# Two half-batch groups per weight tile against one group of up to 512 tokens, in an attention and two-layer MLP kernel

## The chip, the cores and the metric

The kernel runs on one core of one Trainium2 chip. Its time is the device time of one execution in microseconds, the median of three executions. Every matrix product is on TensorE (PE); VectorE (DVE), ScalarE (ACT) and GpSimd (POOL) do the elementwise work, and all transfers are issued from SyncE's queue (SP).

## The reference

Four batches of 576 tokens, eight heads of 64. Causal attention with a decay per position gives 2304 tokens of 512 channels, which two MLP layers take in turn.

```python
scores = scale * (q @ k.T) + cum[:, None] - cum[None, :]     # causal; cum = cumsum(log(f))
x = softmax(scores) @ v                                      # heads side by side: 2304 x 512
x = ((x @ w_a) * (x @ w_b)) @ w_out                          # layer 0; 512 -> 1536 -> 512
xn = x / sqrt(mean(x * x) + 1e-6) * rms_g
out = (silu(xn @ w_gate) * (xn @ w_val)) @ w_out2            # layer 1; 512 -> 1536 -> 512
```

## The kernel before, in words

**Phases.** The MLP is cut into chunks of tokens; before, a chunk is a batch. A phase is one layer on one chunk, and `PHASES` (line 32) lists eight of them as (layer, chunk): (0,0), (0,1), (1,0), (0,2), (1,1), (0,3), (1,2), (1,3). Below, "phase 0" to "phase 7" count along this list. A phase goes through 36 weight tiles (`NG`, line 46): 24 for the two inner products, taken by turns (the first of a pair is gated, the second multiplies it), and 12 for the outer product, three to each of four output blocks. Each layer has 36 tiles, so every phase streams all 36 of its layer again.

**Groups.** A bank of PSUM holds 512 fp32 columns, and a batch has 576 tokens, so each chunk is worked in two groups of tokens: `CUT` (line 23) makes them 256 and 320 for batch 0, 288 and 288 for the others. For one weight tile and one group PE does a *block*: 12 matmuls (`block` in `plan_mlp`, lines 571 to 578), four slices of 128 by three products, because operands are split into a high and a low part (`w[0]*xh + w[0]*xl + w[1]*xh`). Each matmul loads its own weights. A block writes one of `M_BANKS` = 4 banks called `m` (line 62); the bank is free again when ACT or DVE has read it (`gate`, `product`, `out_1`, `out_2`).

**Weight tiles.** A tile is 512 KB. On first use it is loaded as 64-bit words (`raw`), decoded (`weights`, lines 480 to 539: ACT `rebase`, DVE `shift` and `join`, ACT `high`, POOL `low`) and saved to DRAM (`wd`); later uses load the saved form, `w<-wd`, line 496. Both live in a ring of `W_BUFS` = 5 buffers. During phase 1, `EARLY[1]` = 16 tiles of layer 1 are decoded ahead of their phase.

**Attention** of a batch is planned into phases by `ATT` (line 40): batch 2 over phases 1 and 2, batch 3 over phases 3 and 4. Scores go to `S_BANKS` = 2 banks `s` (line 1102, and 1124 for the last 64 rows of two heads together), then softmax, transposes to one bank `t` (line 804), products with V to one bank `pv` (line 1185). Phase 0 starts after a special start-up for the first 256 rows of batch 0, with three banks `bm`.

**Order.** All operations are recorded first and then put in a fixed order per engine by a list scheduler (`Plan.order`, line 212) with costs such as `mm` (line 67) and due times from `block_time`. Each engine then runs its list strictly in order: an instruction that waits holds up all behind it.

Of the kernel before, what the change touches and what calls it, by code (L numbers as in the profile page):

```python
# [9 lines left out]
F32 = mybir.dt.float32  # L10
F32R = mybir.dt.float32r
# [10 lines left out]

CUT = (256, 288, 288, 288)
N0, NMAX = CUT[0], max(max(x, S - x) for x in CUT)
PIECES = sorted({0, S, *CUT})
NEG = -8e9
# [4 lines left out]

PHASES = [(0, 0), (0, 1), (1, 0), (0, 2), (1, 1), (0, 3), (1, 2), (1, 3)]

LAG = 18
SLOT = [0, 1, 2, 0]

EARLY = {0: 1, 1: 16}

# [3 lines left out]
    (1, ALL, ((0, LAG, 99, 1.0),), 2),  # L42
    (2, ALL, ((1, 0, 99, 0.7), (2, 0, 99, 0.5)), 0),
    (3, ALL, ((3, 0, 99, 0.4), (4, 0, 99, 0.5)), 0),
]
# [7 lines left out]

AHEAD = [18000, 20000, 14000, 20000]
BOOT_STEP, EARLY_AT = 3000, 10000
# [5 lines left out]
W_BUFS, W32_BUFS, A_BUFS, BP_BUFS = 5, 2, 4, 4  # L61
S_BANKS, T_BANKS, PV_BANKS, M_BANKS = 2, 1, 1, 4
P_BUFS, PT_BUFS = 4, 4
LANDED, READY, RATE = 980, 230, 360


def mm(n):

    return max(107.0, n / 2.4 + 12.5)

# [15 lines left out]
def dve(n):  # L86
    return 69 + n / 0.96
# [10 lines left out]
def pool1(n):  # L98
    return 55 + n / 0.96
# [6 lines left out]
def half(c, s):  # L106

    return slice(CUT[c] * s, S if s else CUT[c])


def size(c, s):
    return S - CUT[c] if s else CUT[c]


def halves_of(c, a, e):
    return [s for s in range(2) if a < half(c, s).stop and e > half(c, s).start]

# [184 lines left out]
class Kernel:  # L302
# [91 lines left out]
    def make_x(self, pool, s):  # L394
        for t in range(2):
            for k in range(KT):
                self.X[s, t, k] = pool.tile([128, S], F32R, name=f"x{s}{t}{k}")

# [15 lines left out]
    def steps(self, p):  # L414

        both = (0, 1)
        if p:
            return [(j, both) for j in range(NG)]
        ab = 2 * FT
        return (  # L420
            [(j, both[:1]) for j in range(LAG)] + [(j, both) for j in range(LAG, ab)]
            + [(j, both[1:]) for j in range(LAG)] + [(j, both) for j in range(ab, NG)]
        )

    def weave(self):
        np_ = len(PHASES)
        blocks = [sum(len(subs) for _, subs in self.steps(p)) for p in range(np_)]
        extra = [[0.0] * n for n in blocks]
        for c, rows, parts, sf in ATT:
            for p, a, e, share in parts:  # L430
                span = range(a, min(e, blocks[p]))
                for i in span:
                    extra[p][i] += share * sum(self.unit_cost(u, h < sf) for u in rows for h in range(H)) / len(span)

        self.T, t = [], 0.0
        for p in range(np_):
            self.T.append([t])
# [13 lines left out]
        todo, norm = list(ATT), None
        for p, (m, c) in enumerate(PHASES):
            while todo and todo[0][2][0][0] <= p:
                self.plan_attention(*todo.pop(0))
            self.plan_mlp(p, m, c, norm)
            norm = (p, c) if m == 0 else None
# [85 lines left out]
    def plan_mlp(self, p, m, c, norm):  # L542
# [3 lines left out]
        for i_step, (j, subs) in enumerate(self.steps(p)):  # L546
            w = self.weights(m, j, self.block_time(p, k + 1))
            if i_step % 3 != 1:
                for i in early:
                    self.weights(1, i, self.block_time(p, k + 1) + 20000)  # L550
                    break
            if norm and i_step == 0:
                stages = self.plan_norm(*norm)
            if norm and i_step in NORM_STEPS:
                next(stages)
            for s in subs:
# [116 lines left out]
    def out_2(self, acc, c, i, s, e):  # L673
        nc, op = self.nc, self.op
        o, n = self.tile([128, NMAX], "a", A_BUFS), size(c, s)
        t0 = c * S + half(c, s).start
        op(
# [9 lines left out]
    def plan_norm(self, p, c):  # L687
        parts = self.x_parts[1, c] = []
        for s in range(2):
            self.normed(c, s, self.block_time(p + 1, NORM_AT + 4 * s), parts)  # L690
            yield
# [159 lines left out]
    def first_pair(self, i, u, t):  # L851
# [6 lines left out]
        cols = [slice(g * e, g * e + e) for g in range(2)]  # L858
        s = self.bank("bm", 3, (128, 512), self.bpsum)
        p = self.tile([128, 2 * N0], "bP", BP_BUFS, pool=self.bp)  # L860
# [149 lines left out]

    def plan_attention(self, c, rows, spread, sf):
        spans = [(self.T[p][a], self.T[p][min(e, len(self.T[p]) - 1)], share) for p, a, e, share in spread]
        spans[-1] = (spans[-1][0], spans[-1][1] - AHEAD[c], spans[-1][2])

        def place(x):
            for a, b, share in spans:
                if x <= share:
                    break
                x -= share
            return a + (b - a) * x / share  # L1020

        *whole, last = rows
# [4 lines left out]
        after = [n for s in range(2) for n in self.ab_blocks.get((1, 0, s), [])] if c == 3 else []  # L1027
        for hs in zip(range(0, H, 2), range(1, H, 2)):
            f = hs[1] < sf
            tiles = [self.head(c, h, rows[0][0], place(pos / total), f) for h in hs]  # L1030
            groups = [[last], *(whole[i : i + 2] for i in range(0, len(whole), 2))]
            for us in groups:
                pss = []
                for u in us:
# [5 lines left out]
                    pos += 2 * weigh(rows.index(u), u, hs[0])  # L1040
                self.values(c, hs, us, pss, tiles, t, after)

    def head(self, c, h, q0, t, sf):

# [18 lines left out]
        vr = self.tile([128, 5, D], "vr", 4)  # L1063
        load(256 * (S - q0), lambda: qr.tile[0:64, q0:], self.qT[g, :, q0:], writes=[(qr, 0)], dt=15000)
        load(147456, lambda: kr.tile[0:64], self.kT[g], writes=[(kr, 0)], dt=15000)
        for x, i in zip((qb, kb), at):
# [63 lines left out]

    def values(self, c, hs, us, pss, tiles, t, after):

# [45 lines left out]
        def product(x):  # L1178
# [14 lines left out]
        )  # L1193
        late = ["late"] if SLOT[c] == 2 else []
        out = lambda i: self.X[SLOT[c], i, hs[0] // 2][:, a0:e1]
        hi, lo = (("xb", c, i, hs, a0) for i in range(2))
        n = e1 - a0
        op(
            ACT, act(n, 1), lambda: nc.scalar.activation(out(0), pv.tile[:, :n], AF.Copy), reads=[pv, *late], writes=[hi],
            prio=t + 6500, after=after,  # L1200
        )
        op(
            DVE, dve(n),
            lambda: nc.vector.tensor_tensor(out=out(1), in0=pv.tile[:, :n], in1=out(0).bitcast(F32), op=ALU.subtract),
            reads=[pv, hi, *late], writes=[lo], prio=t + 6800, after=after,
        )
        self.x_parts.setdefault((0, c), []).extend([(hi, halves_of(c, a0, e1)), (lo, halves_of(c, a0, e1))])


# [48 lines left out]
```

## Time and profile before

| | us |
|---|---|
| median of three runs | 1142.66 |
| lowest, highest | 1137.82, 1145.03 |
| the profiled execution | 1149.22 |
| its span, first to last instruction | 1147.4 |

The span is cut in stretches below at the phase borders of this execution: start-up to 36, phase 0 to 254, phase 1 to 398, phase 2 to 530, phase 3 to 660, phase 4 to 800, phase 5 to 914.5, phase 6 to 1029.5, phase 7 to the end. A PE matmul's shown duration includes its way through the array and overlaps the next one, so the cost of a matmul is read from the distance between starts.

### The profile page before, as it was taken

Reading aid. Unit: us, or ns where it says so; the run is one execution under the profiler, and the core shown is the slowest. Engines: PE = TensorE matmul, PEld = TensorE weight load, DVE = VectorE, ACT = ScalarE, POOL = GpSimd, SP = SyncE. Lnnn points to the kernel's source line nnn. Section 1 sums busy time; section 2 is a strip of 40 time slices with the busy share of each in tenths; the row PEclk is TensorE's granted clock in tenths of the full one; section 3 lists DMA queues with packets and bytes.
Section 4 is the critical chain, followed back from the end, with each engine's and each line's share of the span. In section 5 each row is a group of like instructions: output and inputs, shape, how many; then the busy total and the mean of one; then the engine's idle time right before and its main releaser. Section 6 shows DMA issues by size and latency. Waiting matters only on the chain.

```text
span 1147.4 us, 22605 instructions
## 1 busy us (share of the span) xinstructions
PE 1129.9 (98%) x8742; PEld 1084.2 (94%) x8742; DVE 562.9 (49%) x1587; ACT 490.3 (43%) x1208; POOL 180.3 (16%) x187
## 2 busy tenths in 40 slices
PE   8999999999999999999999999999999999999998
PEld 7676899999999999999999999999999999999998
DVE  5567757667973469642352268621221166204420
ACT  6677647666663446542342245422222133112210
POOL 2323313432421012441020020200000000000000
PEclk7889999999999999999999999999999999999999
DMA  6768796879797454697455454445555555565553
GB/s 184 241 215 297 275 293 220 265 229 320 251 377 219 142 159 157 224 316 259 148 163 162 149 161 148 141 157 157 169 166 166 166 165 165 170 197 173 166 174 107
DMA packets 77184, 229.82 MB, mean 200 GB/s; under 512 B 11533, under 2 KB 22493, under 8 KB 77077
## 3 DMA queue, kind: packets, MB, share of 16 engines
q1 hardware_dynamic: 77076, 228.38, 61.2%
q8 instruction: 69, 1.13, 0.4%
q14 instruction: 39, 0.31, 0.1%
HBM read 185.21 MB, written 43.13 MB: 199 GB/s over the span
## 4 chain that ended last, share of the span: by engine, by line
PE 86%; DMA 6%; ACT 3%; DVE 2%; issue 1%; POOL 1%; SPq 0%; ACTq 0%; DVEq 0%; POOLq 0%
PE m L576 25%; PE m L578 24%; PE m L577 24%; PE pv L1185 3%; PE t L804 3%; PE s L1102 3%; DMA raw<-wb 2%; PE s L1124 2%; DMA raw<-wo 1%; ACT P L769 1%; DMA kr<-kT 1%; DMA bq<-aux 1%; ACT w L515 1%; DVE w L523 1%; DMA raw<-wv 0%
## 5 line engine op out<-in xcount | busy, mean ns | idle before, releaser
L576 PE MATMUL m<-x,w 128*128 128x288 f32 (+2 forms) x1536 | 462.6, 301 | 0.0
L578 PE MATMUL m<-x,w 128*128 128x288 f32 (+2 forms) x1536 | 453.8, 295 | 0.1
L577 PE MATMUL m<-x,w 128*128 128x288 f32 (+2 forms) x1536 | 453.1, 295 | 0.0
L576 PEld LDWEIGHTS m<-x,w 128*128 128x128 f32 x1536 | 289.4, 188 | 5.1 <-issue 3.0
L577 PEld LDWEIGHTS m<-x,w 128*128 128x128 f32 x1536 | 289.6, 189 | 0.8 <-issue 0.2
L578 PEld LDWEIGHTS m<-x,w 128*128 128x128 f32 x1536 | 289.1, 188 | 0.3 <-POOL w L490 0.3
L576 PE MATMUL m<-g,w 128*128 128x288 f32 (+2 forms) x768 | 229.4, 299 | 0.0
L578 PE MATMUL m<-g,w 128*128 128x288 f32 (+2 forms) x768 | 226.6, 295 | 0.0
L577 PE MATMUL m<-g,w 128*128 128x288 f32 (+2 forms) x768 | 226.3, 295 | 0.0
L634 ACT ACTIVATE g<-a 128x288 fp32r<-128x288 f32 (+2 forms) x192 | 84.7, 442 | 174.0 <-DVE a L618 173.7
L618 DVE TENSOR_TENSOR a<-m,a 128x288 f32<-128x288 f32 (+2 forms) x192 | 87.3, 455 | 125.6 <-PE m L578 119.7
L576 PEld LDWEIGHTS m<-g,w 128*128 128x128 f32 x768 | 144.5, 188 | 1.5 <-issue 1.2
L577 PEld LDWEIGHTS m<-g,w 128*128 128x128 f32 x768 | 144.6, 188 | 0.1
L578 PEld LDWEIGHTS m<-g,w 128*128 128x128 f32 x768 | 144.4, 188 | 0.0
L490 POOL TENSOR_TENSOR w<-w,w 128x512 fp32r<-128x512 f32 x72 | 99.1, 1383 | 208.5 <-ACT w L487 147.5
L600 ACT ACTIVATE a<-m 128x288 f32<-128x288 f32 (+2 forms) x192 | 78.1, 407 | 120.3 <-PE m L578 119.7
L637 DVE TENSOR_TENSOR g<-a,g 128x288 fp32r<-128x288 f32 (+2 forms) x182 | 91.9, 506 | 58.9 <-ACT g L634 58.4
L769 ACT ACTIVATE P<-P,mn 128x512 f32<-128x512 f32 (+4 forms) x128 | 76.3, 597 | 43.5 <-DVE mn L762 42.4
L762 DVE CUSTOM_DVE_ANT_0 P<-s,mask 128x512 f32<-128x512 f32 (+4 forms) x128 | 61.9, 498 | 65.2 <-PE s L1102 46.2
L607 DVE SCALAR_TENSOR_TENSOR a<-a,m 128x288 f32<-128x288 f32 (+1 forms) x96 | 43.1, 452 | 93.7 <-ACT a L600 93.4
L1166 ACT ACTIVATE pt<-t 128x384 f32<-128x384 f32 (+2 forms) x101 | 51.6, 511 | 43.7 <-PE t L804 43.6
L804 PE MATMUL t<-ident,P 128*128 128x128 f32 (+1 forms) x376 | 63.2, 278 | 6.5 <-ACT pt L1166 6.1
(105 smaller groups left out, 1065.8 us busy)
## 6 DMA issues: line engine op xcount, KB each, us to landing
w<-wd SPq DMA_DIRECT2D x251, 512.0 KB
wd<-w SPq DMA_DIRECT2D x72, 512.0 KB
raw<-wo SPq DMA_DIRECT2D x24, 512.0 KB
raw<-wa SPq DMA_DIRECT2D x12, 512.0 KB
raw<-wb SPq DMA_DIRECT2D x12, 512.0 KB
raw<-wg SPq DMA_DIRECT2D x12, 512.0 KB
raw<-wv SPq DMA_DIRECT2D x12, 512.0 KB
vr<-vA SPq DMA_DIRECT2D x32, 128.0 KB
```

The source lines that it names most:

```text
L490: nc.gpsimd.tensor_tensor(out=w.tile[:, 1, :], in0=i32.tile.bitcast(F32), in1=w.tile[:, 0, :].bitcast(F32), op=ALU.subtract)
L576: nc.tensor.matmul(o, w.tile[:, 0, wc], xh, start=kt == 0, stop=False)
L577: nc.tensor.matmul(o, w.tile[:, 0, wc], xl, start=False, stop=False)
L578: nc.tensor.matmul(o, w.tile[:, 1, wc], xh, start=False, stop=kt == last)
L600: ACT, act(n, 1), lambda x: nc.scalar.activation(x[:, :n], acc.tile[:, :n], func, scale=scale),
L618: nc.vector.tensor_tensor(out=a.tile[:, :n], in0=acc.tile[:, :n], in1=a.tile[:, :n], op=ALU.mult)
L634: nc.scalar.activation(out(0), x(), AF.Copy, **({} if scale is None else {"scale": scale}))
L637: self.engine(by).tensor_tensor(out=out(1), in0=x(), in1=out(0).bitcast(F32), op=ALU.subtract)
L762: nc.vector.tensor_tensor_reduce(out=p.tile[:n, i * w : i * w + w], in0=s[i].tile[:n, :w], in1=masks[i][:n], scale=-0.125, scalar=mn.tile[ ...
L769: nc.scalar.activation(o, o, AF.Exp, bias=mn.tile[:n, len(s) - 1 : len(s)], scale=-1.0, accum_out=x[:n])
L804: nc.tensor.transpose(ps.tile[:w, c : c + n], p.tile[:n, i * 128 : i * 128 + w], self.ident[:n, :n])
L1166: nc.scalar.activation(x.tile[:r, :to], ps.tile[:r, :to], AF.Copy)
```

## The change

Batch 0 keeps its two groups. The other 1728 tokens are cut without regard to batches into chunks of 512, 448, 320 and 448, each worked as a single group, so there are ten phases of 36 tiles instead of eight; the (layer, chunk) list is given in the diff. Phases are again counted from 0, so phase 1 is now layer 0 on 512 tokens, and phase 8 layer 1 on 320. Attention of batches 2 and 3 is planned in two parts each and loads only the keys that a part needs; results that fall into two chunks are copied in two pieces (`homes`). There are three `s` banks, three `m` banks and two `bm` banks, instead of two, four and three. The planner's matmul cost and its DMA rate are other numbers, and 14 tiles instead of 16 are decoded early, evenly over phase 1.

```diff
-CUT = (256, 288, 288, 288)
-N0, NMAX = CUT[0], max(max(x, S - x) for x in CUT)
+CHUNKS = [(0, (256, 320)), (576, (512,)), (1088, (448,)), (1536, (320,)), (1856, (448,))]
+WIDTH = [sum(x) for _, x in CHUNKS]
...
-PHASES = [(0, 0), (0, 1), (1, 0), (0, 2), (1, 1), (0, 3), (1, 2), (1, 3)]
+PHASES = [(0, 0), (0, 1), (1, 0), (0, 2), (1, 1), (0, 3), (1, 2), (0, 4), (1, 3), (1, 4)]
...
-SLOT = [0, 1, 2, 0]
-
-EARLY = {0: 1, 1: 16}
+
+SLOT, HAD = [0, 1, 2, 0, 1], {3: 0, 4: 1}
+
+EARLY = {0: 1, 1: 14}
...
-    (2, ALL, ((1, 0, 99, 0.7), (2, 0, 99, 0.5)), 0),
-    (3, ALL, ((3, 0, 99, 0.4), (4, 0, 99, 0.5)), 0),
+    (2, ALL[:3], ((1, 0, 99, 0.6), (2, 0, 99, 0.5)), 0),
+    (2, ALL[3:], ((3, 0, 99, 0.7), (4, 0, 99, 0.4)), 0),
+    (3, ALL[:1], ((4, 18, 99, 1.0),), 0),
+    (3, ALL[1:], ((5, 0, 99, 0.6), (6, 0, 99, 0.5)), 0),
...
-S_BANKS, T_BANKS, PV_BANKS, M_BANKS = 2, 1, 1, 4
+S_BANKS, T_BANKS, PV_BANKS, M_BANKS, BM_BANKS = 3, 1, 1, 3, 2
 P_BUFS, PT_BUFS = 4, 4
-LANDED, READY, RATE = 980, 230, 360
+LANDED, READY, RATE = 980, 230, 320
 
 
 def mm(n):
 
-    return max(107.0, n / 2.4 + 12.5)
+    return max(107.0, 0.4375 * n + 7)
...
-            if i_step % 3 != 1:
+            if p == 1 and (i_step + 1) * EARLY[1] // NG > i_step * EARLY[1] // NG:
...
-        s = self.bank("bm", 3, (128, 512), self.bpsum)
+        s = self.bank("bm", BM_BANKS, (128, 512), self.bpsum)
```

What moves is shown at three places. The first is PE in a phase without attention, at the border between two blocks; `m` is the bank written, `x` the activations, `w` the weight tile. Before, in the last phase (layer 1, batch 3):

```order
L576 MATMUL m2142_12993<-x003_115,w2141_12870 128x288
L577 MATMUL m2142_12993<-x013_119,w2141_12870 128x288
L578 MATMUL m2142_12993<-x003_115,w2141_12870 128x288
L576 MATMUL m2144_13011<-x000_112,w2141_12870 128x288
L577 MATMUL m2144_13011<-x010_116,w2141_12870 128x288
L578 MATMUL m2144_13011<-x000_112,w2141_12870 128x288
```

and with the change in phase 8:

```order
L591 MATMUL m2123_11058<-x003_115,w2119_10993 128x320
L592 MATMUL m2123_11058<-x013_119,w2119_10993 128x320
L593 MATMUL m2123_11058<-x003_115,w2119_10993 128x320
L591 MATMUL m2126_11077<-x000_112,w2125_11011 128x320
L592 MATMUL m2126_11077<-x010_116,w2125_11011 128x320
L593 MATMUL m2126_11077<-x000_112,w2125_11011 128x320
```

Before, the weight tile stays for a second block; now each block has a new tile.

The second place is SP's queue in phase 1, where stored tiles of layer 0 (`w<-wd`), raw tiles of layer 1, saves (`wd<-w`) and loads of attention heads go out by turns. Before:

```order
L496 DMA w_3921<-wd_9_147 128x1024
L512 DMA raw_3926<-wv 128x512
L528 DMA wd_6_180<-w_3910 128x1024
L496 DMA w_4002<-wd_10_148 128x1024
L496 DMA w_4046<-wd_11_149 128x1024
L512 DMA raw_4061<-wg 128x512
```

and with the change, at the same stored tiles:

```order
L511 DMA w_3696<-wd_9_147 128x1024
L511 DMA w_3718<-wd_10_148 128x1024
L527 DMA raw_3739<-wg 128x512
L511 DMA w_3742<-wd_11_149 128x1024
L543 DMA wd_3_177<-w_3752 128x1024
L511 DMA w_3786<-wd_12_150 128x1024
```

At the same point of the phase three fewer saves have gone out; the early tiles are spread further back.

The third place is PE at the start, at the first scores (`bm`) and the idle matmuls that fill waits (`warm`). Before:

```order
L817 MATMUL warm_212<-spun 128x128 x13
L868 MATMUL bm_242<-bk,bq 128x128 x2
L868 MATMUL bm_250<-bk,bq 128x256 x2
L868 MATMUL bm_264<-bk,bq 128x128 x2
L868 MATMUL bm_271<-bk,bq 128x256 x2
```

and with the change:

```order
L832 MATMUL warm_212<-spun 128x128 x13
L883 MATMUL bm_242<-bk,bq 128x128 x2
L883 MATMUL bm_250<-bk,bq 128x256 x2
L883 MATMUL bm_264<-bk,bq 128x128 x2
L832 MATMUL warm_212<-spun 128x128
L883 MATMUL bm_276<-bk,bq 128x256 x2
```

The fourth pair of scores now stands behind an idle matmul, since its bank is one that an earlier pair used.

## Rows read from the trace of the kernel before

**Rows 1.** The page: span, PE, and granted PE clock in 40 slices.

```profile
span 1147.4 us, 22605 instructions
PE 1129.9 (98%) x8742; PEld 1084.2 (94%) x8742; DVE 562.9 (49%) x1587; ACT 490.3 (43%) x1208; POOL 180.3 (16%) x187
PEclk7889999999999999999999999999999999999999
```

**Rows 2.** Stretches by phase: busy us (instructions) per engine, clock, DMA share, GB/s.

```profile
36.00:254.00 218.00, 210.16 (x1634) 182.35 (x1634) 144.59 (x440) 140.28 (x340) 70.50 (x71) 0.97 0.78 256
254.00:398.00 144.00, 142.68 (x1148) 138.61 (x1148) 91.49 (x261) 79.02 (x196) 38.27 (x37) 1.00 0.77 262
398.00:530.00 132.00, 130.74 (x1029) 128.77 (x1027) 82.26 (x205) 67.12 (x155) 42.30 (x38) 1.00 0.67 226
...
800.00:914.50 114.50, 114.50 (x867) 114.50 (x866) 24.29 (x53) 26.12 (x64) 0.00 (x0) 1.00 0.54 168
```

**Rows 3.** Timeline of PE, phase 2: start us, duration us; first matmuls of successive blocks.

```profile
500.11 0.28 PE L576 MATMUL m<-g,w 128*128 128x256 f32 x1
...
501.55 0.31 PE L576 MATMUL m<-g,w 128*128 128x320 f32 x1
...
503.31 0.28 PE L576 MATMUL m<-g,w 128*128 128x256 f32 x1
```

**Rows 4.** Timeline of PE: four score matmuls in a row, twice, and what follows.

```profile
289.31 0.40 PE L1102 MATMUL s<-ka,qa 128*128 128x512 f32 x1
...
290.24 0.30 PE L576 MATMUL m<-x,w 128*128 128x288 f32 x1
...
775.86 0.34 PE L1102 MATMUL s<-ka,qa 128*128 128x384 f32 x1
...
776.57 0.29 PE L576 MATMUL m<-g,w 128*128 128x288 f32 x1
```

**Rows 5.** PE's waits in the whole span: us in total, times, longest.

```profile
PE t L804 <- ACT pt L1166: 6.1, 7, 1.5
PE s L1124 <- POOL ka L1049: 2.4, 2, 1.6
...
PE s L1102 <- DVE mn L762: 0.4, 2, 0.2
```

**Rows 6.** Stretches chosen by DMA load; columns as in rows 2.

```profile
60.00:230.00 170.00, 164.09 (x1318) 144.71 (x1315) 116.04 (x353) 110.38 (x270) 51.87 (x51) 0.99 0.80 262
254.00:350.00 96.00, 95.41 (x763) 92.75 (x763) 76.16 (x208) 63.77 (x154) 32.53 (x29) 1.00 0.88 308
320.00:335.00 15.00, 15.00 (x133) 14.35 (x132) 10.35 (x29) 9.36 (x23) 3.86 (x3) 1.00 1.02 417
```

**Rows 7.** Waits of SP's queue in the whole span: the longest.

```profile
SPq L496 <- PE m L578: 469.2, 180, 5.1
```

**Rows 8.** Timelines of PE, ACT and DVE, end of phase 2's inner products.

```profile
487.16 0.31 PE L578 MATMUL m<-x,w 128*128 128x320 f32 x1
...
490.51 0.28 PE L576 MATMUL m<-g,w 128*128 128x256 f32 x1
...
489.52 0.67 ACT L515 ACTIVATE w<-raw 128x512 f32<-128x512 f32 x1 [2.16 <-DMA raw<-wo]
490.09 0.42 ACT L600 ACTIVATE a<-m 128x320 f32<-128x320 f32 x1
...
490.54 0.49 DVE L607 SCALAR_TENSOR_TENSOR a<-a,m 128x320 f32<-128x320 f32 x1 [1.35 <-ACT a L600]
```

**Rows 9.** Groups by line in phase 2: busy, mean ns, idle before, releaser.

```profile
L515 ACT ACTIVATE w<-raw 128x512 f32<-128x512 f32 x18 | 12.1, 674 | 20.4 <-DMA raw<-wo 17.3 <-DMA raw<-wv 2.3 <-DMA raw<-wg 0.8
```

**Rows 10.** Timeline of the end: the last matmul and the last copy.

```profile
1143.85 0.29 PE L578 MATMUL m<-g,w 128*128 128x288 f32 x1
...
1144.23 0.41 ACT L678 ACTIVATE a<-m 128x288 f32<-128x288 f32 x1 [1.18 <-PE m L578]
```

More of the change, by code (lines that the diff above doesn't have):

```diff
@@ L21 @@
 KT, FT = DM // 128, DFF // 128
-CUT = (256, 288, 288, 288)
-N0, NMAX = CUT[0], max(max(x, S - x) for x in CUT)
-PIECES = sorted({0, S, *CUT})
+CHUNKS = [(0, (256, 320)), (576, (512,)), (1088, (448,)), (1536, (320,)), (1856, (448,))]
+WIDTH = [sum(x) for _, x in CHUNKS]
+N0, NMAX = CHUNKS[0][1][0], max(max(x) for _, x in CHUNKS)
+PIECES = sorted({0, N0, *WIDTH})
 NEG = -8e9
@@ L52 @@
 SCAN_2, AU_AT, PEN = 8500, 16000, 100
-AHEAD = [18000, 20000, 14000, 20000]
+AHEAD = [18000, 20000, 14000, 20000, 14000, 20000]
 BOOT_STEP, EARLY_AT = 3000, 10000
@@ L106, in half, with homes @@
 def half(c, s):
-    return slice(CUT[c] * s, S if s else CUT[c])
+    a = sum(CHUNKS[c][1][:s])
+    return slice(a, a + size(c, s))
 def size(c, s):
-    return S - CUT[c] if s else CUT[c]
+    return CHUNKS[c][1][s]
 def halves_of(c, a, e):
-    return [s for s in range(2) if a < half(c, s).stop and e > half(c, s).start]
+    return [s for s in range(len(CHUNKS[c][1])) if a < half(c, s).stop and e > half(c, s).start]
+def homes(b, a, e):
+    a, e = b * S + a, b * S + e
+    for c, (x, _) in enumerate(CHUNKS):
+        i, j = max(a, x), min(e, x + WIDTH[c])
+        if i < j:
+            yield c, slice(i - x, j - x), slice(i - a, j - a)
 def pieces(c, s, *key):
@@ L396, in make_x @@
             for k in range(KT):
-                self.X[s, t, k] = pool.tile([128, S], F32R, name=f"x{s}{t}{k}")
+                n = max(w for w, x in zip(WIDTH, SLOT) if x == s)
+                self.X[s, t, k] = pool.tile([128, n], F32R, name=f"x{s}{t}{k}")
     def make_g(self, pool, fs):
@@ L414, in steps @@
     def steps(self, p):
-        both = (0, 1)
+        both = tuple(range(len(CHUNKS[PHASES[p][1]][1])))
         if p:
@@ L453, in weave @@
             while todo and todo[0][2][0][0] <= p:
-                self.plan_attention(*todo.pop(0))
+                self.plan_attention(AHEAD[-len(todo)], *todo.pop(0))
             self.plan_mlp(p, m, c, norm)
@@ L554, in plan_mlp @@
             if norm and i_step in NORM_STEPS:
-                next(stages)
+                next(stages, None)
             for s in subs:
@@ L675, in out_2 @@
         o, n = self.tile([128, NMAX], "a", A_BUFS), size(c, s)
-        t0 = c * S + half(c, s).start
+        t0 = CHUNKS[c][0] + half(c, s).start
         op(
@@ L688, in plan_norm @@
         parts = self.x_parts[1, c] = []
-        for s in range(2):
+        for s in range(len(CHUNKS[c][1])):
             self.normed(c, s, self.block_time(p + 1, NORM_AT + 4 * s), parts)
@@ L1008, in cumulative, with plan_attention @@
         )
-    def plan_attention(self, c, rows, spread, sf):
+    def plan_attention(self, ahead, c, rows, spread, sf):
         spans = [(self.T[p][a], self.T[p][min(e, len(self.T[p]) - 1)], share) for p, a, e, share in spread]
-        spans[-1] = (spans[-1][0], spans[-1][1] - AHEAD[c], spans[-1][2])
+        spans[-1] = (spans[-1][0], spans[-1][1] - ahead, spans[-1][2])
         def place(x):
@@ L1020, in place @@
             return a + (b - a) * x / share
-        *whole, last = rows
+        last = rows[-1] if rows[-1][1] - rows[-1][0] < 128 else None
+        whole = [u for u in rows if u != last]
         weigh = lambda i, u, h: 1200 + self.unit_cost(u, h < sf) + (1000 if i == 0 else 0)
@@ L1025, in plan_attention @@
         pos = 0.0
-        after = [n for s in range(2) for n in self.ab_blocks.get((1, 0, s), [])] if c == 3 else []
         for hs in zip(range(0, H, 2), range(1, H, 2)):
             f = hs[1] < sf
-            tiles = [self.head(c, h, rows[0][0], place(pos / total), f) for h in hs]
-            groups = [[last], *(whole[i : i + 2] for i in range(0, len(whole), 2))]
+            tiles = [self.head(c, h, rows[0][0], rows[-1][1], place(pos / total), f) for h in hs]
+            groups = [*([[last]] if last else []), *(whole[i : i + 2] for i in range(0, len(whole), 2))]
             for us in groups:
@@ L1040, in plan_attention, with head @@
                     pos += 2 * weigh(rows.index(u), u, hs[0])
-                self.values(c, hs, us, pss, tiles, t, after)
-    def head(self, c, h, q0, t, sf):
+                self.values(c, hs, us, pss, tiles, t)
+    def head(self, c, h, q0, k1, t, sf):
         nc, op = self.nc, self.op
@@ L1063, in head @@
         vr = self.tile([128, 5, D], "vr", 4)
-        load(256 * (S - q0), lambda: qr.tile[0:64, q0:], self.qT[g, :, q0:], writes=[(qr, 0)], dt=15000)
-        load(147456, lambda: kr.tile[0:64], self.kT[g], writes=[(kr, 0)], dt=15000)
+        load(256 * (k1 - q0), lambda: qr.tile[0:64, q0:k1], self.qT[g, :, q0:k1], writes=[(qr, 0)], dt=15000)
+        load(256 * k1, lambda: kr.tile[0:64, :k1], self.kT[g, :, :k1], writes=[(kr, 0)], dt=15000)
         for x, i in zip((qb, kb), at):
@@ L1070, in head @@
             )
-        load(131072, lambda: vr.tile[:, 0:4, :], self.vA[g], writes=[(vr, 0)], dt=11000)
-        load(16384, lambda: vr.tile[0:64, 4, :], self.vB[g], writes=[(vr, 1)], dt=10000)
-        v = [(vr, 0), (vr, 1)]
+        nv = min(k1 // 128, 4)
+        load(32768 * nv, lambda: vr.tile[:, 0:nv, :], self.vA[g, :, 0:nv], writes=[(vr, 0)], dt=11000)
+        v = [(vr, 0)]
+        if k1 > 512:
+            load(16384, lambda: vr.tile[0:64, 4, :], self.vB[g], writes=[(vr, 1)], dt=10000)
+            v.append((vr, 1))
         if sf:
@@ L1077, in head @@
         q, k = (qr, 0), (kr, 0)
-        n = S - q0
-        op(POOL, pool1(n), lambda x: copy(x[0:64, q0:], qr.tile[:, q0:]), reads=[q], writes=[(qa, 0)], prio=t - 9000)
-        op(POOL, pool1(n), lambda: copy(qb.tile[0:64, q0:], qr.tile[:, q0:]), reads=[q], writes=[(qb, 0)], prio=t - 8000)
+        n = k1 - q0
+        op(POOL, pool1(n), lambda x: copy(x[0:64, q0:k1], qr.tile[:, q0:k1]), reads=[q], writes=[(qa, 0)], prio=t - 9000)
+        op(POOL, pool1(n), lambda: copy(qb.tile[0:64, q0:k1], qr.tile[:, q0:k1]), reads=[q], writes=[(qb, 0)], prio=t - 8000)
         op(
-            DVE, dve(n), lambda: rest(qa.tile[64:128, q0:], qr.tile[:, q0:], qa.tile[0:64, q0:]),
+            DVE, dve(n), lambda: rest(qa.tile[64:128, q0:k1], qr.tile[:, q0:k1], qa.tile[0:64, q0:k1]),
             reads=[q, (qa, 0)], writes=[(qa, 1)], prio=t - 7000, port=True,
         )
-        op(POOL, pool1(S), lambda x: copy(x[0:64], kr.tile), reads=[k], writes=[(ka, 0)], prio=t - 7000)
-        op(POOL, pool1(S), lambda: copy(ka.tile[64:128], kr.tile), reads=[k], writes=[(ka, 1)], prio=t - 6000)
+        op(POOL, pool1(k1), lambda x: copy(x[0:64, :k1], kr.tile[:, :k1]), reads=[k], writes=[(ka, 0)], prio=t - 7000)
+        op(POOL, pool1(k1), lambda: copy(ka.tile[64:128, :k1], kr.tile[:, :k1]), reads=[k], writes=[(ka, 1)], prio=t - 6000)
         op(
-            DVE, dve(S), lambda: rest(kb.tile[0:64], kr.tile, ka.tile[0:64]),
+            DVE, dve(k1), lambda: rest(kb.tile[0:64, :k1], kr.tile[:, :k1], ka.tile[0:64, :k1]),
             reads=[k, (ka, 0)], writes=[(kb, 0)], prio=t - 5000, port=True,
@@ L1129, in packed, with values @@
         return p, None
-    def values(self, c, hs, us, pss, tiles, t, after):
+    def values(self, c, hs, us, pss, tiles, t):
         nc, op = self.nc, self.op
@@ L1193, in values, with high, low @@
         )
[L1194 to L1207, printed above, removed]
+        for ch, cols, rs in homes(c, a0, e1):
+            late = ["late"] if SLOT[ch] == 2 else []
+            after = [x for s in range(len(CHUNKS[HAD[ch]][1])) for x in self.ab_blocks[1, HAD[ch], s]] if ch in HAD else []
+            hi, lo = (("xb", ch, i, hs, a0) for i in range(2))
+            n = rs.stop - rs.start
+            out = lambda i, ch=ch, cols=cols: self.X[SLOT[ch], i, hs[0] // 2][:, cols]
+            def high(out=out, rs=rs):
+                nc.scalar.activation(out(0), pv.tile[:, rs], AF.Copy)
+            def low(out=out, rs=rs):
+                nc.vector.tensor_tensor(out=out(1), in0=pv.tile[:, rs], in1=out(0).bitcast(F32), op=ALU.subtract)
+            op(ACT, act(n, 1), high, reads=[pv, *late], writes=[hi], prio=t + 6500, after=after)
+            op(DVE, dve(n), low, reads=[pv, hi, *late], writes=[lo], prio=t + 6800, after=after)
+            parts = self.x_parts.setdefault((0, ch), [])
+            parts.extend([(hi, halves_of(ch, cols.start, cols.stop)), (lo, halves_of(ch, cols.start, cols.stop))])
 def tile_kernel(tc, *args):
```

## The prediction, made before the changed kernel was run

> **What bounds the kernel now.** I read the page first: PE is busy for 1129.9 of 1147.4 us, and its clock is granted in full but for the first slices [rows 1]. So the question is what each matmul costs and where PE still waits. The stretches by phase answer the second: in phase 5, without attention, PE has no idle time and 864 matmuls take 114.5 us, 132.5 ns each; phase 1, with attention, idles for 1.3 us in 144; only phase 0 has idle time worth naming, 218.0 - 210.2 = 7.8 us [rows 2]. The list of PE's waits agrees: 6.1 us for copies of transposes, 2.4 us for a copied key, 0.4 us before scores [rows 5]. The kernel is bound by PE's stream of matmuls; the change can gain by making the same columns cheaper per column, and lose by making PE wait for something that now is hidden.
>
> **The change, part by part.**
>
> *Matmuls of the MLP.* A layer has 36 tiles of 12 matmuls, so each token group is visited 2 x 432 = 864 times. Before there are eight groups: 256, 320 and six of 288; afterwards six: 256, two of 320, two of 448, one of 512. Columns are the same, 2304; 1728 matmuls go. What this is worth depends on how the distance between matmuls grows with width. By starts of blocks of twelve, 256 columns take (501.55 - 500.11)/12 = 120.0 ns and 320 take (503.31 - 501.55)/12 = 146.7 ns [rows 3]; 288 takes 132.5 [rows 2]. No row shows an MLP matmul wider than 320. The nearest are scores, four in a row: 384 columns (776.57 - 775.86)/4 = 177.5 ns, 512 columns (290.24 - 289.31)/4 = 232.5 ns [rows 4]. The eight groups cost 120.0 + 146.7 + 6 x 132.5 = 1061.7 ns per matmul of a tile. Three readings for the six:
> - The line through 256 and 320 (0.417 ns per column): 448 takes 200.1 and 512 takes 226.8; sum 1040.4, a gain of 21.3 ns x 864 = 18.4 us. This is the low end.
> - Strictly by columns at 288's 0.460 ns: 206.1 and 235.6; sum 1061.2, a gain of 0.4 us. This is the high end.
> - The line through 256 and the measured 512 (0.4395): 448 takes 204.4; sum 120.0 + 2 x 146.7 + 2 x 204.4 + 232.5 = 1054.7, a gain of 7.0 ns x 864 = 6.0 us.
>
> I take the third, because it rests on the one row that has the width in question. So there is little fixed cost per matmul to save.
>
> The Trainium skill, "TensorE: Matmul & The Clock Gate", section on the back-to-back issue gap, gives N/2.4 + 2.5 ns for a warm matmul, which speaks against a large gain: two groups fewer would save 2 x 2.5 x 864 = 4.3 us, an estimate from that page. The trace doesn't bear out its level: it would make 288 columns 122.5 ns, and the row has 132.5.
>
> *Attention.* The order has the same number of score, transpose and V matmuls. Batches 2 and 3 load and copy each head in two parts: 16 more small sets of loads on SP's queue and of copies on POOL and DVE. POOL is busy for 180 of 1147 us and DVE for 49% [rows 1]; I cost these at 0, covered by matmuls, and at the 2.4 us that PE waited for such copies in all [rows 5] if the cover fails as often again.
>
> *Three product banks instead of four.* The third block after a given one must now find its bank read. Where that is tight, a 320-wide block issues its last matmul at 487.16 [rows 8]. ACT's queue then stands 2.16 us at a decode that waits for its raw tile, the gate behind it starts at 490.09, and DVE is through with the bank at 490.54 + 0.49 = 491.03. The third block after (two blocks of 256 and 320 lie between) starts at 490.51: it would wait about 0.5 us. ACT stands 20.4 us at such decodes in phase 2, in 18 cases [rows 9]; if a few hit such a place, some 4 us are lost, the high end. Outside phases 0 and 2 a block of a single group lasts 12 x 146.7 ns = 1.8 us at least, mostly 2.5 to 2.8, without a second group in between, and I see no shortage. I take +1.
>
> *Three score banks, two start-up banks.* PE waited 0.4 us before scores [rows 5], so as a wait removed this is nothing. The order of phase 0 changes, though, and there lie 7.8 us of idle time [rows 2]: ends -7.8 and +3 (half of PE's waits for transposes again), taken as -1. At the start a pair of scores stands behind one idle matmul; 0, at most the 1 us of a few more.
>
> *The end.* The last block is 448 wide: ACT's last copy goes from 0.41 us [rows 10] to about 0.64, and the last store from 144 to 224 KB, 0.2 us more at 417 GB/s [rows 6]. +0.4.
>
> *The weight stream.* Two more phases of 36 tiles, less two early ones that are read back: 70 more loads of 0.524 MB. SP's loads of stored tiles waited 469 us for PE to free a buffer [rows 7]: transfers have slack on the whole. The dense places are two. Phase 1: 432 x 232.5 ns = 100.4 us plus 80 attention and norm matmuls, which at the rate of phase 1 before ((144.0 - 114.5) us for 208 of them, 0.14 us each) [rows 2] are 11 us: 112 us. It moves 36 tiles, 14 raw tiles in and 14 out, and 1.4 MB for heads: 35.0 MB, or 313 GB/s. Phase 8: 432 x 146.7 ns = 63.4 us for 36 tiles and 0.66 MB out, 19.5 MB, or 308 GB/s. Before, 308 GB/s ran for 96 us at a DMA share of 0.88 with PE idle for 0.6 us, and 417 GB/s for 15 us with none [rows 6]. So both fit, just; 0.
>
> Sum: -6.0 + 0 + 1 - 1 + 0.4 + 0 = -5.6, about -6 us on the profiled execution of 1149.2 us. That one is 6.6 us over the median of 1142.66, with nothing in it that the change touches in another proportion, so I forecast 1142.66 - 6 = **1136.5 us**.
>
> **The rivals.**
>
> *Wide matmuls are cheap (faster).* If width costs what the line through 256 and 320 says, the MLP gains 18.4 us; with part of phase 0's idle time that gives 1122 to 1126. For it: scores alternate between operands of 128 and 68 rows [rows 4], which an MLP block does not, and may overstate 512. Against it: 384 and 512 columns both lie above that line. Readings between it and mine fall under 1131 from a gain of 12 us on.
>
> *The weight stream falls behind (slower).* One mechanism: phases 1 and 8 ask for 313 and 308 GB/s, and if the stream gives less, PE waits for tiles. At the 262 GB/s of the stretch from 60 to 230 [rows 6], phase 1 would last 35.0/0.262 = 133.6 us, +22, and phase 8 74.4 us, +11: 1142.7 - 6 + 33 = 1170 us. It decides as soon as the rate stays under some 310 GB/s, and outweighs the gain from about 295. For it: a share of 0.88 is near full, and by proportion phase 5's 168 GB/s at 0.54 [rows 2] gives only 311. Against it: the 417 GB/s [rows 6], and that the 262 were at a share of 0.80, so asked for rather than the limit.
>
> The Trainium skill, "DMA: Bandwidth & Descriptors", in its anatomy of a DMA on the gpsimd path, fits 2.0 us plus bytes at 436 GB/s, and under its measured bandwidths asks for 1 MiB per transfer. A tile would then take 3.2 us (an estimate) against phase 8's 1.76 us per tile, and one after the other they would add some 52 us there. The trace says that they overlap: fifteen microseconds at 417 GB/s.
>
> *Small waits eat the gain (no change).* Three banks in phase 2 at +4, a worse order in phase 0 at +3, copies at +2: 1142.7 - 6 + 9 = 1146; one or two of them give 1139 to 1144.
>
> **How the numbers follow.** Forecast 0.46 (gain between 2 and 11 us: 1132 to 1141), cheap wide matmuls 0.30 (1120 to 1131), small waits 0.14 (1140 to 1147), weight stream 0.10 (1150 to 1170). The range 1123 to 1147 leaves out the stream's rival and the far tail of the cheap one. About 1% (11.4 us) is what can be told from no change here. Faster by more than that, under 1131.2: the cheap rival and a little of the forecast, 0.31. Slower, over 1154.1: the stream, 0.09. Within: 0.60.
>
> **What would show it.** In phases 8 and 9 of the new profile, without attention, the length of 432 matmuls gives 320 and 448 columns directly: 63.4 and 88.3 us by my reading, 86.4 for 448 in the cheap case. Phase 1 near 112 us with PE idle under 2 us shows the stream right; waits of PE's weight loads for DMA there or in phase 8 show the rival. Phase 2's idle time over its 132.0 - 130.7 = 1.3 us [rows 2] shows the third bank missing. Phase 0's length against 218 us shows what the order did. The prediction is wrong if 448 or 512 columns in a block cost under 200 or over 237 ns, or if any phase grows by idle time.

## The result, and the profile after

The changed kernel takes 1123.1 us (four runs, 1122.6 to 1128.3) against 1141.2 us for the kernel before (four runs): ratio 0.986, 95% interval 0.982 to 0.989. In a second comparison with more runs it is 1127.1 against 1138.0 us, ratio 0.990 (0.987 to 0.993). So it is faster by about 1.1%, some 12 us. The forecast had -6 us and 1136.5; the first median lies at the very edge of its range, and the gain is above the 2 to 11 us that the forecast gave its own mechanism. One execution in the table below, of the kernel with the old DMA rate, ran in a slower state of the chip and is left out of its row.

The page of the changed kernel, to be read beside [rows 1]:

```profile
span 1120.8 us, 19350 instructions
PE 1109.3 (99%) x7012; PEld 999.3 (89%) x7012; DVE 556.8 (50%) x1481; ACT 466.4 (42%) x1076; POOL 198.7 (18%) x245
PEclk9999999999999999999999999999999999999999
```

1730 matmuls are gone, 1728 of them the MLP's, and PE is still busy throughout. The weight loads' busy share fell from 94% to 89%: a load lasts 188 ns in both traces, and wider matmuls leave room between loads. The clock line differs from that of before, which began with 7, 8, 8. That is not the change's work, as the second traces of both kernels show below.

Stretches of the changed kernel, cut at its phase borders (start-up, phases 0, 1, 2 and 7 to 9; columns as in [rows 2]):

```profile
0.00:29.50 29.50, 27.86 (x184) 21.79 (x184) 20.33 (x85) 23.20 (x68) 10.48 (x17) 1.00 0.78 230
29.50:236.40 206.90, 202.98 (x1630) 179.30 (x1630) 145.45 (x452) 137.53 (x335) 70.16 (x68) 0.99 0.81 268
236.40:347.20 110.80, 110.26 (x538) 89.84 (x538) 65.98 (x169) 54.39 (x120) 26.85 (x30) 1.00 0.87 300
347.20:473.90 126.70, 125.86 (x963) 124.06 (x962) 80.07 (x184) 63.91 (x141) 40.40 (x39) 1.00 0.76 259
...
877.70:965.30 87.60, 87.60 (x434) 81.20 (x433) 16.27 (x26) 16.98 (x31) 0.00 (x0) 1.00 0.70 220
965.30:1029.50 64.20, 64.04 (x436) 63.74 (x435) 27.66 (x56) 17.52 (x37) 0.00 (x0) 1.00 0.86 293
1029.50:1116.90 87.40, 87.40 (x434) 80.99 (x432) 22.45 (x36) 15.57 (x28) 0.00 (x0) 1.00 0.69 212
```

Phase 9 is 432 matmuls of 448 columns in 87.4 us: 202.3 ns each. Phase 8, 320 columns at 293 GB/s, lasts 64.2 us with 0.16 us of idle time; the stream kept up. So it did in phase 1: 300 GB/s, 0.5 us idle. The timeline of PE in phase 1 gives 512 columns, in a quiet stretch and in one beside attention (start us, duration us):

```profile
243.87 0.39 PE L591 MATMUL m<-x,w 128*128 128x512 f32 x1
...
246.59 0.39 PE L591 MATMUL m<-x,w 128*128 128x512 f32 x1
...
250.24 0.40 PE L591 MATMUL m<-x,w 128*128 128x512 f32 x1
...
252.99 0.28 PE L1119 MATMUL s<-ka,qa 128*128 128x256 f32 x1
```

Twelve matmuls take 2.72 us, 226.7 ns each, or 2.75 us, 229.2 ns. Over all distances inside blocks of this trace, the first of each block left out, the mean is 228.5. Behind attention the first is longer, 297 ns on average. The scores of [rows 4] had said 232.5.

PE's waits in the changed kernel, beside [rows 5]:

```profile
PE s L1141 <- DMA kb<-aux: 1.5, 2, 0.9
PE t L819 <- ACT pt L1183: 1.4, 2, 0.8
PE m L591 <- DVE a L633: 1.0, 2, 0.8
```

The third row is not in [rows 5]: an MLP block that waited until DVE had read its bank. How far the missing fourth bank is behind it is taken up below. And the weight stream's queue still waits for PE far more than the other way round, as in [rows 7]:

```profile
SPq L511 <- PE m L593: 392.9, 216, 4.1
```

### The profile page after: what moved, and what is told of

Read it like the earlier page. It is cut to its first block, busy times and chain, and to the rows that moved or that the text cites. A ratio compares the mean times of both kernels' runs of the same rounds, so it can differ in the third digit from the quotient of the medians.

```text
span 1120.8 us, 19350 instructions
## 1 busy us (share of the span) xinstructions
PE 1109.3 (99%) x7012; PEld 999.3 (89%) x7012; DVE 556.8 (50%) x1481; ACT 466.4 (42%) x1076; POOL 198.7 (18%) x245
## 4 chain that ended last, share of the span: by engine, by line
PE 92%; DVE 4%; DMA 2%; ACT 1%; issue 0%; SPq 0%; POOL 0%; ACTq 0%; POOLq 0%
PE m L591 26%; PE m L593 26%; PE m L592 26%; PE pv L1202 4%; PE t L819 3%; PE s L1119 3%; PE s L1141 2%; PE warm L832 1%; DMA kb<-aux 1%; DMA raw<-wb 1%; DMA raw<-wa 0%; DMA qr<-qT 0%; DVE P L777 0%; DVE x L761 0%; DVE x L655 0%
## 5 line engine op out<-in xcount | busy, mean ns | idle before, releaser
L591 PE MATMUL m<-x,w 128*128 128x320 f32 (+3 forms) x1152 | 399.0, 346 | 1.2 <-DVE a L633 1.0
L593 PE MATMUL m<-x,w 128*128 128x320 f32 (+3 forms) x1152 | 388.3, 337 | 0.0
L592 PE MATMUL m<-x,w 128*128 128x320 f32 (+3 forms) x1152 | 388.0, 337 | 0.0
L591 PEld LDWEIGHTS m<-x,w 128*128 128x128 f32 x1152 | 217.1, 188 | 20.3 <-issue 4.7
L593 PEld LDWEIGHTS m<-x,w 128*128 128x128 f32 x1152 | 216.9, 188 | 13.8
L592 PEld LDWEIGHTS m<-x,w 128*128 128x128 f32 x1152 | 217.3, 189 | 13.1 <-issue 0.5
L591 PE MATMUL m<-g,w 128*128 128x320 f32 (+3 forms) x576 | 197.5, 343 | 0.0
L593 PE MATMUL m<-g,w 128*128 128x320 f32 (+3 forms) x576 | 194.1, 337 | 0.0
L592 PE MATMUL m<-g,w 128*128 128x320 f32 (+3 forms) x576 | 194.0, 337 | 0.0
L633 DVE TENSOR_TENSOR a<-m,a 128x320 f32<-128x320 f32 (+3 forms) x144 | 79.7, 555 | 175.2 <-PE m L593 167.5
L649 ACT ACTIVATE g<-a 128x320 fp32r<-128x320 f32 (+3 forms) x144 | 75.0, 521 | 157.3 <-DVE a L633 157.1
L615 ACT ACTIVATE a<-m 128x320 f32<-128x320 f32 (+3 forms) x144 | 70.3, 489 | 112.3 <-PE m L593 111.0
L591 PEld LDWEIGHTS m<-g,w 128*128 128x128 f32 x576 | 108.6, 188 | 8.0 <-issue 1.2
L593 PEld LDWEIGHTS m<-g,w 128*128 128x128 f32 x576 | 108.5, 188 | 6.8
L592 PEld LDWEIGHTS m<-g,w 128*128 128x128 f32 x576 | 108.6, 189 | 6.4
L652 DVE TENSOR_TENSOR g<-a,g 128x320 fp32r<-128x320 f32 (+3 forms) x139 | 84.4, 608 | 50.5 <-ACT g L649 49.7
L1183 ACT ACTIVATE pt<-t 128x384 f32<-128x384 f32 (+4 forms) x105 | 51.5, 490 | 58.4 <-PE t L819 57.7
L622 DVE SCALAR_TENSOR_TENSOR a<-a,m 128x256 f32<-128x256 f32 (+3 forms) x72 | 39.7, 551 | 62.3 <-ACT a L615 60.6
```

What stands on the lines that cost most here:

```text
L591: nc.tensor.matmul(o, w.tile[:, 0, wc], xh, start=kt == 0, stop=False)
L592: nc.tensor.matmul(o, w.tile[:, 0, wc], xl, start=False, stop=False)
L593: nc.tensor.matmul(o, w.tile[:, 1, wc], xh, start=False, stop=kt == last)
L615: ACT, act(n, 1), lambda x: nc.scalar.activation(x[:, :n], acc.tile[:, :n], func, scale=scale),
L633: nc.vector.tensor_tensor(out=a.tile[:, :n], in0=acc.tile[:, :n], in1=a.tile[:, :n], op=ALU.mult)
L649: nc.scalar.activation(out(0), x(), AF.Copy, **({} if scale is None else {"scale": scale}))
```

## The experiments

**A second trace of the kernel before.** No edit.

> The unchanged kernel once more, for a second trace of it. The profiled execution of before was 8 us over its median, and 17.7 us of the 26.6 us between the two profiled spans lie in start-up and phase 0, which keep their two groups. Theory 'chance' (those 17.7 us are the disturbed execution: PE's clock was at half for 27 us there): start-up and phase 0 end near 240 us, within 4 us of the changed kernel's 236. Theory 'order' (banks or order make start-up and phase 0 shorter): they end at 244 to 250 us again. Under both, phases 1 to 7 take 890 us as before.

It took 1140.5 us. Its stretches at its own phase borders (start-up, phases 0, 1, 2, and the last):

```profile
0.00:31.50 31.50, 27.12 (x183) 21.48 (x183) 20.55 (x84) 23.54 (x69) 11.09 (x18) 0.98 0.80 226
31.50:245.00 213.50, 208.36 (x1633) 183.57 (x1633) 143.57 (x440) 140.88 (x340) 69.58 (x70) 0.97 0.79 262
245.00:388.00 143.00, 142.41 (x1151) 138.85 (x1149) 91.42 (x261) 79.20 (x197) 39.18 (x37) 1.00 0.78 264
388.00:521.20 133.20, 131.25 (x1026) 128.66 (x1025) 83.64 (x204) 66.76 (x155) 41.62 (x38) 1.00 0.66 221
...
1020.70:1135.10 114.40, 114.40 (x865) 114.40 (x864) 32.89 (x72) 23.88 (x56) 0.00 (x0) 1.00 0.50 158
```

Phase 0 ends at 245.0, as the theory "order" expected, 8.6 us later than in the changed kernel; but also 9 us sooner than in the first trace of the same program. Phases 1 to 7 take 890.1 us, as before. A block waits for its bank here too, with four of them, and the granted clock separates the executions:

```profile
PE m L576 <- DVE a L607: 0.6, 1, 0.6
...
core 0: 1138.7 us, clock 0.994
PEclk9899999999999999999999999999999999999999
```

Each execution of every kernel has its mean clock. Over the 70 distinct runs of the kernel before from all comparisons, time goes with it: a straight line through them gives 1134.0 us at clock 1.000 and 1.13 us more for each 0.001 less. The line leaves a scatter of 2.2 us: runs at 1.000 lie between 1131 and 1137 us, those at 0.990 at 1146. In the two traces of either kernel the clock falls to its lower level of 1.2 GHz in start-up and phase 0, where PE has gaps, for 3 to 27 us in all.

So the table gives, beside medians, the mean over the runs after 1.15 us per 0.001 of missing clock is taken off; its standard error is 0.2 to 0.7 us. The runs come from three comparisons, each on another chip, and on this footing the kernel before stands at 1134.6, 1134.2 and 1132.0 us in them. The last column is therefore the difference from the kernel before in the same comparison, with a standard error of 0.6 to 0.9 us. The change is worth 12.4 us. In the first comparison the changed kernel's four runs had a mean clock of 0.9975, against 0.9958 in the second, which is 2 us; the clocks of the four runs of before are not on record, so what made the rest of that first difference of 18 us is not shown.

| kernel | median us | ratio to before (95%) | at clock 1.000 | less before's |
|---|---|---|---|---|
| before, all 70 runs | 1138.0 | | 1133.9 | |
| changed, first comparison | 1123.1 | 0.986 (0.982 to 0.989) | 1121.4 | |
| changed, second | 1127.1 | 0.990 (0.987 to 0.993) | 1121.8 | -12.4 |
| before, banks 3/3/2 | 1139.8 | 1.000 (0.997 to 1.004) | 1135.7 | +1.1 |
| before, planner's new numbers | 1141.0 | 1.004 (1.001 to 1.007) | 1135.8 | +1.1 |
| changed, banks 2/4/3 | 1127.8 | 0.990 (0.988 to 0.993) | 1124.1 | -10.5 |
| the same, 512 as two of 256 | 1140.1 | 1.002 (0.999 to 1.006) | 1136.4 | +2.2 |
| changed, banks 2/3/3 | 1130.0 | 0.993 (0.990 to 0.996) | 1125.8 | -8.4 |
| changed, both old numbers | 1135.7 | 0.997 (0.993 to 1.000) | 1127.0 | -7.2 |
| changed, old DMA rate | 1136.5 | 0.998 (0.995 to 1.001) | 1127.0 | -5.0 |
| changed, cost laid through the trace | 1129.3 | 0.991 (0.988 to 0.995) | 1122.7 | -9.3 |
| changed, DMA rate 290 | 1128.9 | 0.993 (0.991 to 0.995) | 1123.2 | -8.8 |

(Banks are scores, products, start-up.) Below, "at equal clock" is the last column.

**The changed kernel once more.** No edit.

> The changed kernel once more, in more runs beside the kernel before. Over 25 runs of before, time goes with PE's granted clock: 1134.5 us at clock 1.000 and 1.18 us more for each 0.001 less (least squares). If the change itself makes 13 us (the four runs so far lie at about 1121.7 by the same slope) and the rest of the 18 us was a low clock of before in the first comparison: 1124 to 1127 us, ratio 0.986 to 0.989. If all 18 us are the change's: 1121 to 1123, ratio 0.983 to 0.985.

1127.1 us and 0.990: the first reading, or just beside it. Its profiled execution shows how much the clock does to one program (start-up, phases 0 and 2, and PE's waits for product banks):

```profile
core 0: 1130.7 us, clock 0.990
PEclk8899999999999999999999999999999999999999
...
0.00:34.20 34.20, 31.94 (x185) 25.69 (x185) 20.46 (x85) 24.51 (x69) 11.47 (x19) 0.85 0.78 231
34.20:243.70 209.50, 205.96 (x1630) 180.80 (x1630) 145.97 (x452) 137.21 (x334) 69.31 (x67) 0.98 0.79 259
...
354.90:483.70 128.80, 126.39 (x964) 124.18 (x963) 81.68 (x184) 63.63 (x141) 41.24 (x39) 1.00 0.73 254
...
PE m L591 <- ACT a L693: 1.6, 2, 1.0
PE m L591 <- DVE a L633: 1.0, 2, 0.9
```

Ten microseconds more than the first trace, with the same instructions. Of these, 7.3 lie before phase 1, where the clock was low, and 2.1 in phase 2, where PE idles for 2.4 us and not 0.8.

**The banks alone.**

```diff
-S_BANKS, T_BANKS, PV_BANKS, M_BANKS = 2, 1, 1, 4
+S_BANKS, T_BANKS, PV_BANKS, M_BANKS = 3, 1, 1, 3
-        s = self.bank("bm", 3, (128, 512), self.bpsum)
+        s = self.bank("bm", 2, (128, 512), self.bpsum)
```

> The kernel before with the banks of the change alone: three score banks, three product banks, two start-up banks; chunks, phases and planner numbers as before. If the banks shorten start-up and phase 0: 6 to 9 us faster than before, 1132 to 1135 us, with the first MLP matmul near 30 us. If only the width of the groups counts: within 3 us of before, or up to 4 us slower in phase 2 where a third bank is short.

No gain: 1.000, and 1.1 us worse at equal clock, little more than the noise. A wait of the kind that the forecast named, for a product bank in phase 2, appears in its list:

```profile
PE m L576 <- ACT a L678: 2.3, 1, 2.3
```

**The chunks with the old banks.** On the changed kernel, with its planner's numbers:

```diff
-S_BANKS, T_BANKS, PV_BANKS, M_BANKS, BM_BANKS = 3, 1, 1, 3, 2
+S_BANKS, T_BANKS, PV_BANKS, M_BANKS, BM_BANKS = 2, 1, 1, 4, 3
```

> The changed kernel with the banks of before: two score, four product and three start-up banks; chunks, phases and planner numbers as changed. If width alone makes the gain: within 3 us of the changed kernel, 1120 to 1126 us. If the banks give the 6 to 7 us that the price of wide matmuls (11.7 us by the new trace) leaves over: 1129 to 1132 us.

The median, 1127.8, falls between the two readings; at equal clock it gains 10.5 us, 1.9 less than the changed kernel. No run has the new chunks with both the old banks and the planner's old numbers, so what the chunks are worth alone was not measured.

**The planner's numbers alone.**

```diff
-    return max(107.0, n / 2.4 + 12.5)
+    return max(107.0, 0.4375 * n + 7)
-LANDED, READY, RATE = 980, 230, 360
+LANDED, READY, RATE = 980, 230, 320
```

> The kernel before with the planner's two new numbers alone (matmul cost 0.4375 n + 7, DMA rate 320): only the order moves. If the order by those numbers is what shortens phase 0: 3 to 8 us faster than before. If width and banks are all: within 3 us of before.

Nothing gained: 1.004, 1.1 us worse at equal clock. In the old chunks the old order was no worse.

**One width changed.** On the last but one, the changed kernel with the old banks:

```diff
-CHUNKS = [(0, (256, 320)), (576, (512,)), (1088, (448,)), (1536, (320,)), (1856, (448,))]
+CHUNKS = [(0, (256, 320)), (576, (256, 256)), (1088, (448,)), (1536, (320,)), (1856, (448,))]
```

> The chunks of the change with the banks of before (2, 4, 3), and the chunk of 512 worked in two groups of 256, so that phases, chunks and weight stream stay and only the width of one group changes. If the gain is the price of wide matmuls (256: 120.0 ns, 512: 229.3 ns in blocks): 864 x (240.0 - 229.3) = 9 us slower than the same kernel with one group of 512, so 1136 to 1138 us. By the forecast's 232.5 ns for 512: 6.5 us slower, 1134 to 1135. If matmuls cost by columns alone and the gain comes from elsewhere (fewer drains, other order): within 2 us, 1126 to 1130.

12.7 us slower at equal clock, more than the 10.5 that this kernel had gained. In the traces the two phases on this chunk last 117.1 and 115.5 us, against 110.8 and 111.0 with one group of 512: 10.8 us. By the prices of 120.0 and 228.5 ns it should be 9.9 us; phases, chunks and weight stream are the same. So the width of one group decides over that much, and the gain does not come from where the chunks or phases lie. What makes the 2 to 3 us beyond the price stays open: the edit also doubles the number of blocks to be drained in these phases, and the order is planned anew.

**Two score banks, three product banks.**

```diff
-S_BANKS, T_BANKS, PV_BANKS, M_BANKS, BM_BANKS = 3, 1, 1, 3, 2
+S_BANKS, T_BANKS, PV_BANKS, M_BANKS, BM_BANKS = 2, 1, 1, 3, 3
```

> The changed kernel with two score banks, three product banks and three start-up banks; one bank stays unused. If the third score bank gives what the banks give together (about 3 us at equal clock): as with two, four and three, 1126 to 1129 us, or up to 2 us more for the product bank that is missing. If the product banks or the start-up make it: 1122 to 1125 us.

1130.0 us, and a gain of 8.4 us at equal clock: 2.1 less than with four product banks, 4.0 less than the changed kernel. The third score bank, with the start-up of two, is worth some 4 us here, and the missing product bank costs some 2. Each is near what these comparisons can tell.

**The planner's old numbers in the changed kernel**, both, and then the rate alone:

```diff
-    return max(107.0, 0.4375 * n + 7)
+    return max(107.0, n / 2.4 + 12.5)
-LANDED, READY, RATE = 980, 230, 320
+LANDED, READY, RATE = 980, 230, 360
```

> The changed kernel with the planner's old numbers (n/2.4 + 12.5, rate 360): the order alone moves. The planner then takes 512 columns for 225.8 ns instead of 231 and plans loads closer. If order by the new numbers is part of the gain: 2 to 6 us slower than the changed kernel, 1126 to 1131. If not: within 2 us of it.

> The changed kernel with the old DMA rate (360) and the new matmul cost. If the rate carries the 5 us between old and new numbers: 1126 to 1128 at clock 1, median 1130 to 1134. If the matmul cost does: 1121 to 1123 at clock 1, as the changed kernel.

With both old numbers 5.2 us of the gain are lost at equal clock, with the old rate alone 7.4: the rate carries all of it, the matmul cost brings nothing that shows. Their mean clocks were 0.993 in both, where all others had 0.995 to 0.998, so their medians are some 9 us over the changed kernel's 1127.1: an order that expects loads too early seems to make PE lose clock more often, too. In the old chunks with the old banks the same number made nothing better, so its worth depends on what is around it.

**Other numbers.**

```diff
-    return max(107.0, 0.4375 * n + 7)
+    return max(107.0, 0.4255 * n + 11)
```

> The changed kernel with a planner's matmul cost laid through the distances that the new trace shows for 256, 320, 448 and 512 columns (0.4255 n + 11); DMA rate 320. At equal clock the changed kernel stands at 1121.7 us and with both old numbers at 1127.0. If a truer matmul cost makes a better order: 1118 to 1121 at clock 1, a median of 1122 to 1126. If orders that differ by so little scatter by chance: anywhere within 3 us of the changed kernel, on either side.

```diff
-LANDED, READY, RATE = 980, 230, 320
+LANDED, READY, RATE = 980, 230, 290
```

> The changed kernel with a still lower DMA rate in the planner, 290, so that it counts on later landings. If a lower rate helps because transfers in start-up and phase 0 land late: 1118 to 1121 at clock 1. If 320 already covers what lands late: within 2 us of the changed kernel. If it only scatters: on either side, within 4 us.

At equal clock they gain 9.3 and 8.8 us, some 3 us less than the changed kernel. No version beats it.

## Why the prediction was right, and where its size was off

*What bounds it, and the sign*: right. PE stayed busy for 99% of the span, and most of the gain came from the price of its matmuls. That the number lies inside the range is in part luck. The first median is 0.1 us from its lower end, and by size the outcome belongs to the rival of cheap wide matmuls, which held the gains from 12 us on at 0.30, and not to the forecast at 0.46. The forecast also started from 1142.66, where the median of the 70 runs is 1138.0.

*The term that was mis-sized* is the MLP's: the third reading, -6.0 us, taken "because it rests on the one row that has the width in question". By the new rows 448 columns cost 202.3 ns, not 204.4, and 512 cost 228.5, not 232.5. The six groups come to 120.0 + 2 x 146.7 + 2 x 202.3 + 228.5 = 1046.5 ns, so the gain is 15.2 x 864 = 13.1 us. The row for 512 was one of scores, and a score matmul of this width takes longer than one in a block. The text named that as the argument for the cheap rival and then did not let it move the value. The line through 256 and 320, rows of the very kind of matmul that was to be priced, missed 448 and 512 by only 2.2 and 1.7 ns. The truth lies between the two lines, nearer to the cheap one. What makes scores dearer wasn't tried; it stays open.

*Small waits*: right in size, with a spread. After phase 0 PE idles for 2.5 us in the second trace of before (0.6 + 1.9 us in phases 1 and 2, none later), and for 2.4 and 4.3 us in the two traces of the changed kernel. The third product bank, forecast at 1 us, shows as waits of 1.0 and 2.6 us in the lists, and as some 2 us by the runs. Phase 2's idle time, the forecast's sign for it, is 0.8 and 2.4 us against 1.3 and 1.9 before. It does not settle the matter, since with four product banks and the new chunks it is 2.0 us too.

*Where some of the 13.1 us went.* After phase 0 the changed kernel needs 1116.9 - 236.4 = 880.5 us in its first trace and 883.1 in its second, the kernel before 889.9 and 890.1: a gain of 7 to 9.6. The main part of the difference is attention, which the forecast costed at 0 by counting matmuls. By the distances between starts, 880 matmuls of attention and norm after phase 0 take 75 us in both traces of before, and 79 and 80 us in those of the changed kernel. Scores take 32 to 33 us where they took 29; 188 of them stand where 184 stood, and some wait for a copied key, 0.9 us in phase 4. Products with V take 28 us where they took 27: attention in two parts makes 32 groups of them out of 24, and the step from a group's last product to the next matmul is some 185 ns where the others are 49.

*Start-up and phase 0*: taken as -1 within -7.8 and +3; the traces show about -5. They end at 254.0 and 245.0 us before, at 236.4 and 243.7 with the change; -17.6, as the first two read, would have been wrong to explain, as most of it is the clock. The clock was at its lower level for 27 and 14 us before, for 3 and 20 with the change. With half of that taken off, which is an estimate, they end at 240.3 and 238.2, and at 234.7 and 233.4. PE's idle time, which the clock moves less, says the same: 3.8 + 7.8 = 11.6 us and 9.5 before ([rows 2] and the start-up row below), 5.6 and 5.8 with the change. It takes the banks and the rate together: the changed kernel with the old rate idles there for 10.5 us and with the old banks for 11.4 (8.5 with 512 in two groups), the kernel before with either one alone for 9.6 to 10.2. Both together were not tried in the old chunks. The forecast saw the place and the bound, and not the size.

```profile
0.00:36.00 36.00, 32.20 (x183) 25.42 (x183) 20.57 (x84) 24.02 (x69) 10.57 (x17) 0.81 0.66 194
```

*The weight stream*: right. It runs at 300 and 293 GB/s where 313 and 308 were asked for, without a wait of weight loads for DMA that counts. That phase 1 came near the forecast's 112 us is in part luck: the text counted 208 other matmuls in the old phase 1, where the row has 1148 - 864 = 284, and 80 in the new one, where it has 538 - 432 = 106, so its 11 us meet the measured 10.1 by two errors.

*The end*: forecast +0.4. The last matmul and copy, beside [rows 10]:

```profile
1116.90 0.36 PE L593 MATMUL m<-g,w 128*128 128x448 f32 x1
1117.29 0.55 ACT L693 ACTIVATE a<-m 128x448 f32<-128x448 f32 x1 [6.69 <-PE m L593]
```

From the last matmul's start to the end of the span it is 3.9 us, and was 1147.4 - 1143.85 = 3.6.

*The spread*: the sum was made on a profiled execution that was 6.6 us over its median, and the text put that down to nothing. It was the clock for the most part, as its rows already said: 7 to 8 tenths in the first three slices [rows 1]. Its mean was 0.988, against 0.996 over the 70 runs, and by 1.13 us per 0.001 that is 9 us.

## What to carry to other kernels

Price an operation by rows of the same kind of operation, even if their sizes are further away, before rows of another kind at the right size; where the two disagree, the forecast belongs between them. Look at the clock of every execution before two traces are subtracted: here start-up and phase 0, which the change shortens by some 5 us, differed by 18 us in the first two traces, and half of it was gone in the next trace of the same program. PE's idle time in a stretch is moved less by the clock than the stretch's length. In a kernel with a fixed order, a planner's number for transfers can be worth as much as a part of the change itself, and its worth doesn't carry over from one order to the next.

## What the runs showed of the hardware that was not expected

Distances between matmuls of fp32r operands that each load their own 128 x 128 weights, in blocks at full clock: 120.0 ns for 256 columns, 132.5 for 288, 146.7 for 320, 202.3 for 448, 226.7 to 229 for 512. With 512 at its mean of 228.5, a line 0.4255 n + 11 meets all within 1.1 ns. The Trainium skill, "TensorE: Matmul & The Clock Gate", in its section on the back-to-back issue gap, gives N/2.4 + 2.5 ns for a matmul by itself, which would be 109, 122.5, 135.8, 189 and 216 ns, and 131 ns at 512 columns for a stream of loads and matmuls. The trace bears out neither: it lies 10 to 13 ns above the formula at each width. The two groups saved here were worth 1061.7 - 1046.5 = 15.2 ns per matmul of a tile, 7.6 each, where the formula has 2.5.

The run-to-run spread of this kernel, 1131 to 1147 us over 70 runs of one program, goes with the granted clock for two thirds of its variance: 1.13 us for each 0.001 of its mean. Runs at full clock still differ by up to 6 us.
